# Converting float64 words with an integer add on GpSimd, a planner that keeps VectorE's and GpSimd's SBUF steps apart, and scores in two half banks

## Chip, cores and metric

The kernel runs on one core of one Trainium2 chip. The metric is the device time of one execution in microseconds (us), lower is better. An execution is also recorded by the hardware profiler; its span is the time from the first to the last recorded instruction.

## What is computed

Three parts follow one another. The first is attention within chunks of 64 tokens, for 8 batches, 8 heads and 576 tokens of 64 numbers. The second is a soft mixture of experts on the 4608 x 512 result, with 8 experts of 4 slots. The third is a dense layer of 512 to 2048 with softplus, and one back to 512.

```python
scores = scale * np.matmul(q_c, k_c.transpose(0, 1, 2, 4, 3))   # chunks of 64
attn = np.exp(scores - np.max(scores, axis=-1, keepdims=True))
out = np.matmul(attn / (np.sum(attn, axis=-1, keepdims=True) + 1e-09), v_c)
...
logits = x @ phi                                     # 4608 x 32
d = softmax(logits, over tokens)                     # dispatch
slot_input = (d.T @ x).reshape(8, 4, 512)
slot_out[e] = np.maximum(slot_input[e] @ w1[e], 0.0) @ w2[e]
x = softmax(logits, over slots) @ slot_out           # combine
...
h = x @ w_in
g = np.maximum(h, 0.0) + np.log1p(np.exp(-np.abs(h)))
return (g @ w_out).astype(np.float32)
```

The weights w_in (512 x 2048) and w_out (2048 x 512) come as float64. The kernel loads each number as two 32-bit words, a low and a high one, and makes a float32 of the pair on the chip. One such conversion is of a tile of 128 x 512 numbers; there are 16 of w_in, called wi(c, kt) for quarter c of the 2048 hidden columns and row tile kt, and 16 of w_out, wo0 to wo15, four for each quarter.

## The kernel before

Engines are TensorE (PE), VectorE (DVE), ScalarE (ACT), GpSimd (POOL) and SyncE (SP), which issues all DMAs.

**How the order is made.** The work is cut into named steps. Each step has a cost per engine that may run it (table `COST`), steps that it needs, buffers that it takes and gives back, and a rank. `issue()` (from line 66) is a list scheduler that runs at build time: it keeps a clock for each engine, picks the step that can begin first and emits its instructions. The result is one fixed order for each engine, and on the chip each engine runs its order in line and waits where an operand is not there. A different cost, rank, buffer count or choice of engine changes the orders.

**Stage 1, attention and dispatch (0 to 188.4 us).** There are 36 units of 128 tokens by 512 numbers. For a unit u, PE transposes q and k (L389), ACT copies them to SBUF (B, L401), and PE forms the scores (S, L414: 16 products of 64 x 64 into one PSUM tile of two banks, of which 256 columns each are used). VectorE takes the row maxima (m0, L426) and subtracts them (m1, L432), ACT takes the exponential (x, L439), PE transposes the result (C, L447), ACT copies it out (Ce, L452), PE multiplies by v (D, L466), VectorE normalises (L480, L481, L489), PE transposes back (E, L501) and VectorE copies (Ee, L508). Steps F follow for groups of units and add up logits and slot inputs. There is one score buffer (`S=1`).

**Stage 2, experts (188.4 to 247 us).** PE runs the 16 steps H (w1, L909) and the 16 steps SO (w2), for which weights are streamed in. Beside them the combine weights are made (c1 to c6 and d, L783 to L832; GpSimd makes `cr` at L819 and L820) and the conversions of wi0 and wo0 to 3 run. Then VectorE divides by the sums (so0, L958), PE transposes (soT, L967) and quarter 0 of w_in is folded with the expert results into a table Tc (Td L988, wa L1014, wd L1018).

**Stage 3, the dense layers (from 247 us).** There are 72 steps: 18 token tiles t of 256 by four quarters qd. A step n is: h on PE (L1059, four products 128 x 256 into one of two PSUM tiles `ph`), a sign bit on VectorE (ab, L1072), softplus on ACT (L1078), a maximum and sum on VectorE (mx, L1082), a rounded copy on ACT (pa, L1088), the remainder on GpSimd (pb, L1092), and o on PE: 24 products 128 x 512, eight each at L1109, L1111 and L1113, with w_out held as a rounded and a low part. Sums leave PSUM through oc: a first copy on ACT (L1122) or a sum on VectorE (L1125). The order of steps is: quarter 0 of tiles 0 to EARLY - 1, quarter 1 of the same tiles, quarters 0 and 1 of the others tile by tile, then quarters 2 and 3. EARLY is 4, so step 4 is the first that needs quarter 1 of the table (conversions of wi1, then Tp L996, V L1002, U L1006, wa, wd) and wo4 to 7.

**A conversion before.** For the high word: shift and mask into `cvt` (cb0, L319, VectorE), add the sign (cb1, L322, VectorE), cut the exponent out (cb2, L325, VectorE). ACT squares the high word into `cvm` (cx0, L331) and converts the low word to a float (cx1, L333). Then low times exponent and plus `cvt` (cp0 and cp1, both L847, on VectorE or GpSimd), and a guard that makes tiny numbers zero (cg, L345, VectorE). For w_out there follow a rounded cast (ch, L862, ACT or VectorE) and the low part (cl, L866, GpSimd or VectorE). Two buffer sets `cv` exist at first, four once pool `cvb` opens.

Of the kernel before, what the change touches and what calls it, by code (L numbers as in the profile page):

```python
# [29 lines left out]

COST = {
# [96 lines left out]
def kernel(  # L128
# [711 lines left out]
    def st_cx(k, raw, step, e, held):  # L840
        cv_low(V["cv", k], *words(raw()), step)

    def st_cp(k, raw, step, e, held):
        c = V["cv", k]
        lo, hi = words(raw())
        t = c["t"].bitcast(F32)
        tt(e)(out=t if step else lo, in0=lo, in1=t if step else hi,  # L847
              op=ALU.add if step else ALU.mult)

    def st_cg(k, e, held):  # L850
        c = V["cv", k]
# [507 lines left out]
```

## Time and profile before

| | us |
|---|---|
| runs shown | 719.05, 724.36, 725.68 |
| median | 724.36 |
| the profiled execution | 725.34 |
| its span | 723.6 |

The span is 1.74 us shorter than the profiled execution's own time, which is 0.98 above the median. Times in the rows are microseconds from the span's start. In a row of the timeline stand the start, the duration, the engine, the line of the kernel, the operation, output and inputs by the program's names with shape and type, and a count; in brackets the engine's idle time before the row and what ended it. PEclk is the granted clock of TensorE as a share of 2.4 GHz.

### The profile page before, as it was taken

Reading aid. Unit: us, or ns where it says so; the run is one execution under the profiler, and the core shown is the slowest. Engines: PE = TensorE matmul, PEld = TensorE weight load, DVE = VectorE, ACT = ScalarE, POOL = GpSimd, SP = SyncE. Lnnn points to the kernel's source line nnn. Section 1 sums busy time; section 2 is a strip of 40 time slices with the busy share of each in tenths; the row PEclk is TensorE's granted clock in tenths of the full one; section 3 lists DMA queues with packets and bytes.
Section 4 is the critical chain, followed back from the end, with each engine's and each line's share of the span. In section 5 each row is a group of like instructions: output and inputs, shape, how many; then the busy total and the mean of one; then the engine's idle time right before and its main releaser. Section 6 shows DMA issues by size and latency. Waiting matters only on the chain.

```text
span 723.6 us, 14059 instructions
## 1 busy us (share of the span) xinstructions
PE 659.5 (91%) x5831; PEld 519.2 (72%) x5831; DVE 482.4 (67%) x650; ACT 366.8 (51%) x549; POOL 269.1 (37%) x176
## 2 busy tenths in 40 slices
PE   5998988898997786699999999899999999999997
PEld 4776766676544565488687887788888888888886
DVE  1676877766268799869999899954455555554541
ACT  3897887794046365535455455554333333333330
POOL 2000000000146566645455666753444444333331
PEclk8899999999899799599999999999999999999999
DMA  8898999998499605012323001021323132323222
GB/s 171 225 260 233 284 292 256 297 289 336 186 409 414 266 29 172 32 59 106 127 88 116 30 30 59 30 88 58 116 62 113 64 112 73 102 73 101 73 73 58
DMA packets 79582, 107.92 MB, mean 149 GB/s; under 512 B 41888, under 2 KB 60320, under 8 KB 77216
## 3 DMA queue, kind: packets, MB, share of 16 engines
q1 hardware_dynamic: 79520, 107.04, 46.6%
q8 instruction: 46, 0.75, 0.4%
q14 instruction: 16, 0.13, 0.1%
HBM read 88.15 MB, written 18.87 MB: 148 GB/s over the span
## 4 chain that ended last, share of the span: by engine, by line
PE 62%; DVE 19%; ACT 6%; issue 6%; POOL 4%; SPq 1%; DMA 1%; DVEq 0%; POOLq 0%; ACTq 0%
PE trm L1113 13%; PE trm L1109 13%; PE trm L1111 13%; PE ph L1059 3%; ACT T L401 3%; PE tr L389 3%; PE X L466 3%; PE S L414 2%; PE hps L909 2%; DVE cvt L319 2%; PE tr L501 2%; PE tr L447 2%; DVE cvt L322 2%; DVE cvt L345 2%; DVE hTm L1082 2%
## 5 line engine op out<-in xcount | busy, mean ns | idle before, releaser
L1092 POOL TENSOR_TENSOR g<-hTm,g 128x1024 fp32r<-128x1024 f32 (+2 forms) x50 | 115.9, 2320 | 121.1 <-ACT g L1088 117.3
L401 ACT COPY T<-tr 64x512 f32<-64x512 f32 x144 | 89.6, 622 | 18.9 <-PE tr L389 16.9
L1078 ACT ACTIVATE hTm<-hTm 128x1024 f32<-128x1024 f32 (+2 forms) x51 | 51.5, 1011 | 82.8 <-DVE hTm L1072 82.3
L1088 ACT CAST g<-hTm 128x1024 fp32r<-128x1024 f32 (+2 forms) x51 | 51.0, 999 | 73.1 <-DVE hTm L1082 71.8
L1072 DVE TENSOR_SCALAR hTm<-ph 128x1024 uint32<-128x1024 uint32 (+2 forms) x51 | 59.0, 1158 | 39.8 <-PE ph L1059 39.7
L1092 POOL TENSOR_TENSOR g<-siT,g 128x1024 fp32r<-128x1024 f32 (+1 forms) x25 | 59.0, 2358 | 51.4 <-ACT g L1088 51.3
L1082 DVE SCALAR_TENSOR_TENSOR hTm<-ph,hTm 128x1024 f32<-128x1024 f32 (+2 forms) x51 | 59.0, 1159 | 26.0 <-ACT hTm L1078 25.9
L755 POOL MEMSET siT<- 128x1152 f32 x1 | 1.1, 1057 | 182.2 <-PE tr L577 182.2
L1059 PEld LDWEIGHTS ph<-cT,Tc 128*128 128x128 f32 x288 | 45.2, 197 | 20.9 <-issue 6.6
L1059 PE MATMUL ph<-cT,Tc 128*128 128x256 f32 x288 | 49.6, 297 | 10.0 <-DVE hTm L1082 5.5
L1125 DVE TENSOR_TENSOR i<-trm,i 128x512 f32<-128x512 f32 x44 | 30.2, 687 | 33.7 <-PE trm L1113 33.7
L1078 ACT ACTIVATE siT<-siT 128x1024 f32<-128x1024 f32 (+1 forms) x25 | 25.7, 1027 | 42.2 <-DVE siT L1072 42.1
L1072 DVE TENSOR_SCALAR siT<-ph 128x1024 uint32<-128x1024 uint32 (+1 forms) x25 | 29.5, 1179 | 22.3 <-PE ph L1059 22.3
L1088 ACT CAST g<-siT 128x1024 fp32r<-128x1024 f32 (+1 forms) x25 | 25.4, 1015 | 32.8 <-DVE siT L1082 27.4
L426 DVE TENSOR_REDUCE nm<-S 128x8 f32<-128x512 f32 x36 | 24.8, 690 | 24.5 <-PE S L414 24.1
L1082 DVE SCALAR_TENSOR_TENSOR siT<-ph,siT 128x1024 f32<-128x1024 f32 (+1 forms) x25 | 29.5, 1179 | 15.4 <-ACT siT L1078 15.4
L389 PE MATMUL tr<-ident,q 128*128 128x128 f32 x144 | 30.8, 297 | 4.7 <-DMA q<-in_q_dram 3.8
L414 PE MATMUL S<-T 64*64 64x64 f32 x1152 | 27.7, 228 | 7.2 <-issue 3.0
L414 PEld LDWEIGHTS S<-T 64*64 64x64 f32 x1152 | 22.6, 138 | 13.7 <-issue 10.0
L389 PE MATMUL tr<-ident,k 128*128 128x128 f32 x144 | 28.9, 284 | 1.8 <-DMA k<-in_k_dram 1.8
L508 DVE COPY xT<-tr 128x512 f32<-128x512 f32 x36 | 24.7, 687 | 7.8 <-PE tr L501 7.8
L452 ACT COPY P<-tr 128x512 f32<-128x512 f32 x36 | 21.1, 585 | 16.2 <-PE tr L447 15.6
(449 smaller groups left out, 1807.3 us busy)
## 6 DMA issues: line engine op xcount, KB each, us to landing
part<-i SPq DMA_DIRECT2D x18, 512.0 KB, 2.6
i<-part SPq DMA_DIRECT2D x18, 512.0 KB, 3.8
q<-in_q_dram SPq DMA_DIRECT2D x16, 512.0 KB, 4.6
k<-in_k_dram SPq DMA_DIRECT2D x16, 512.0 KB, 5.6
i<-in_moe_w_dram SPq DMA_DIRECT2D x8, 1024.0 KB, 12.0
vbm<-in_v_dram SPq DMA_DIRECT2D x40, 128.0 KB, 5.6
g<-in_moe_w_dram SPq DMA_DIRECT2D x5, 1024.0 KB, 8.4
...
```

Of the source, the lines that this page charges most:

```text
L389: nc.tensor.transpose(c, t[:, 2 * (u % 2) + h, 2 * rr:2 * rr + 2, :].rearrange("p r d -> p (r d)"), ident)
L401: on(e)(out=t[64 * h:64 * h + 64, :, r2, :], in_=p[64 * r2:64 * r2 + 64])
L414: nc.tensor.matmul(out=sp[64 * o:64 * o + 64, b, 64 * i:64 * i + 64], lhsT=qT[64 * h:64 * h + 64, cs], rhs=kT[64 * h:64 * h + 64, cs], sta ...
L1059: nc.tensor.matmul(out=ph(n, a, b)[:, j - a, :], lhsT=K["Tc"][:, f * 128:(f + 1) * 128], rhs=K["cT"][:, t * TT:(t + 1) * TT], start=True, ...
L1072: nc.vector.tensor_scalar(out=scratch(n, a, b).bitcast(U32), in0=ph(n, a, b).bitcast(U32), scalar1=0x80000000, scalar2=None, op0=ALU.bitwi ...
L1078: nc.scalar.activation(out=y, in_=y, func=AF.Softplus)
L1082: nc.vector.scalar_tensor_tensor(out=y, in0=ph(n, a, b), scalar=0.0, in1=y, op0=ALU.max, op1=ALU.add)
L1088: nc.scalar.copy(out=V["gs", n][:, 0, a:b], in_=scratch(n, a, b))
L1092: tt(e)(out=s[:, 1, a:b], in0=scratch(n, a, b), in1=s[:, 0, a:b].bitcast(F32), op=ALU.subtract)
L1109: nc.tensor.matmul(out=po, lhsT=s[:, 0, j, ts_], rhs=wr[:, hs], start=(n in begin and j == 0), stop=False)
L1111: nc.tensor.matmul(out=po, lhsT=s[:, 0, j, ts_], rhs=wr[:, ls], start=False, stop=False)
L1113: nc.tensor.matmul(out=po, lhsT=s[:, 1, j, ts_], rhs=wr[:, hs], start=False, stop=(j == 3 and n in finish))
```

## The change

- A conversion is now: cb0 and cb1 as before (VectorE); cx0 and cx1 turn the low word into an integer of three bits by scaling it with 2^-29, adding 2^23 and taking 2^23 off again (ACT, two passes, in place); cx2 squares the high word in place (ACT); cb2 is the guard and multiplies `cvt` by 1 or 0 (VectorE); cg adds low word and `cvt` as uint32 (GpSimd, always). cp0 and cp1 are gone, `cvm` and pool `cvb` too; there are four `cv` sets from the start.
- `issue()` has a further clock, `port`: a step whose name is in `PORT` and that runs on VectorE or GpSimd begins no earlier than the last such step ended, on either engine, in the plan. `COST` is retuned, Ce and the first copy in oc may also go to VectorE.
- EARLY is 6. Ranks of late conversions come from a table `need`.
- Scores: one PSUM tile of two banks; a unit takes 256 columns of each bank, and `S=2`. Warm-up products W take no score buffer.

Counts in the two programs: conversion passes on VectorE go from 4 x 32 plus ten cp, four cl and two ch to 3 x 32 plus eleven ch; on GpSimd from 38 cp and 12 cl to 32 cg and 16 cl; on ACT from 64 to 96, and 5 ch for 14. Of 36 Ce, 17 go to VectorE; of 36 first copies, 10 do.

```diff
-EARLY = 4
+EARLY = 6
...
-    "cb0": {"DVE": 0.65}, "cb1": {"DVE": 0.74}, "cb2": {"DVE": 0.55}, "cx0": {"ACT": 0.68},
-    "cx1": {"ACT": 0.68}, "cp0": {"DVE": 0.7, "POOL": 1.4}, "cp1": {"DVE": 0.7, "POOL": 1.4},
-    "cg": {"DVE": 0.87}, "ch": {"ACT": 0.62, "DVE": 0.68}, "cl": {"DVE": 0.7, "POOL": 1.3},
+    "cb0": {"DVE": 0.45}, "cb1": {"DVE": 0.7}, "cb2": {"DVE": 0.7}, "cx0": {"ACT": 0.68},
+    "cx2": {"ACT": 0.68},
+    "cx1": {"ACT": 0.68}, "cg": {"POOL": 1.35}, "ch": {"ACT": 0.62, "DVE": 0.7},
+    "cl": {"DVE": 0.7, "POOL": 1.3},
...
+PORT = {"cb0", "cb1", "cb2", "cl", "pb", "c42", "cg", "c6"}
...
+                if s.nm in PORT and e != "ACT":
+                    t = max(t, port)
...
+        if s.nm in PORT and e != "ACT":
+            port = clock[e]
...
         else:
-            nc.vector.tensor_scalar(
-                out=hi, in0=c["t"], scalar1=0xFF800000, scalar2=None, op0=ALU.bitwise_and)
-
-    def cv_low(c, lo, hi, step):
+            t = c["t"].bitcast(F32)
+            nc.vector.scalar_tensor_tensor(
+                out=t, in0=hi, scalar=TINY2, in1=t, op0=ALU.is_ge, op1=ALU.mult)
+
+    def cv_low(lo, hi, step):
         if step == 0:
-            c["m"] = cv_tile(c, "cvm", F32)
-            nc.scalar.activation(out=c["m"], in_=hi, func=AF.Square)
+            nc.scalar.activation(out=lo, in_=lo.bitcast(U32), func=AF.Copy, scale=2.0 ** -29,
+                                 bias=2.0 ** 23)
+        elif step == 1:
+            nc.scalar.activation(out=lo.bitcast(U32), in_=lo, func=AF.Copy, bias=-2.0 ** 23)
         else:
-            nc.scalar.activation(out=lo, in_=lo.bitcast(U32), func=AF.Copy, scale=2.0 ** -52)
+            nc.scalar.activation(out=hi, in_=hi, func=AF.Square)
...
+    s2 = psa.tile([128, 2, 512], F32, name="S")
...
-            sp = V["S", u] = psa.tile([128, 2, 512], F32, tag="S", name="S")
+            j = held["S", u]
+            sp = V["S", u] = s2[:, :, 256 * j:256 * j + 256]
...
-    clock = issue(steps, dict(BUF, tr=4, S=1, X=1, dT=1))
+    clock = issue(steps, dict(BUF, tr=4, S=2, X=1, dT=1))
...
+        nc.gpsimd.tensor_tensor(out=dst, in0=words(raw())[0].bitcast(U32), in1=t, op=ALU.add)
...
-            nc.scalar.copy(out=hold[t][:, 512 * i:512 * i + 512], in_=po)
+            on(e)(out=hold[t][:, 512 * i:512 * i + 512], in_=po)
...
+    need = {1: (0, 0.5), 2: (EARLY + 4, 0.7), 3: (EARLY + 7, 0.7)}
```

How the orders move is shown at three places, each from the program before and then from the changed one, whose lines are numbered a little differently. The first is VectorE at the end of stage 2, up to the division L958 (L956 in the changed kernel); `cvt` is a conversion's buffer, w1a and w1b are raw halves of w_out. Before:

```order
L345 SCALAR_TENSOR_TENSOR cvt_3698<-cvm_3712,cvt_3698 128x512
L345 SCALAR_TENSOR_TENSOR cvt_3734<-cvm_3741,cvt_3734 128x512
L322 SCALAR_TENSOR_TENSOR cvt_3758<-w1b,cvt_3758 128x512
L866 TENSOR_TENSOR w1a<-cvt_3734,w1a 128x512
L325 TENSOR_SCALAR w1b<-cvt_3758 128x512
L345 SCALAR_TENSOR_TENSOR cvt_3758<-cvm_3766,cvt_3758 128x512
L958 TENSOR_SCALAR ts<-sops_3335,rz 128x256
```

The changed order at the same place:

```order
L327 TENSOR_SCALAR cvt_3752<-w1a 128x512
L327 TENSOR_SCALAR cvt_3755<-w1b 128x512
L330 SCALAR_TENSOR_TENSOR cvt_3752<-w1a,cvt_3752 128x512
L330 SCALAR_TENSOR_TENSOR cvt_3755<-w1b,cvt_3755 128x512
L334 SCALAR_TENSOR_TENSOR cvt_3752<-w1a,cvt_3752 128x512
L334 SCALAR_TENSOR_TENSOR cvt_3755<-w1b,cvt_3755 128x512
L956 TENSOR_SCALAR ts<-sops_3292,rz 128x256
```

The guard L345, which reads what GpSimd wrote, stood in front of the division; in the changed order the steps in front read raw words, `cvt` and ACT's squares alone.

The second place is GpSimd from the last conversions of wi1 (w4b, w5b before) to the low part of wo7 (w3b). L847 is a multiply or add of a conversion, L866 a low part, L1092 a subtract pb of stage 3. Before:

```order
L1092 TENSOR_TENSOR g_4039<-hTm,g_4039 128x1024
L847 TENSOR_TENSOR w5b<-w5b 128x512
L847 TENSOR_TENSOR w2a<-w2a 128x512
L847 TENSOR_TENSOR cvt_4042<-w2a,cvt_4042 128x512
L847 TENSOR_TENSOR cvt_4075<-w2b,cvt_4075 128x512
L866 TENSOR_TENSOR w2a<-cvt_4042,w2a 128x512
L866 TENSOR_TENSOR w2b<-cvt_4075,w2b 128x512
L847 TENSOR_TENSOR w3b<-w3b 128x512
L847 TENSOR_TENSOR cvt_4139<-w3b,cvt_4139 128x512
L866 TENSOR_TENSOR w3a<-cvt_4135,w3a 128x512
L866 TENSOR_TENSOR w3b<-cvt_4139,w3b 128x512
L1092 TENSOR_TENSOR g_4210<-hTm,g_4210 128x1024
```

The changed order, with L855 the integer add and L1090 the subtract pb, from wo4 on:

```order
L855 TENSOR_TENSOR cvt_4034<-w2a,cvt_4034 128x512
L1090 TENSOR_TENSOR g_4091<-siT,g_4091 128x1024
L866 TENSOR_TENSOR w2a<-cvt_4034,w2a 128x512
L855 TENSOR_TENSOR cvt_4095<-w2b,cvt_4095 128x512
L866 TENSOR_TENSOR w2b<-cvt_4095,w2b 128x512
L855 TENSOR_TENSOR cvt_4143<-w3a,cvt_4143 128x512
L1090 TENSOR_TENSOR g_4201<-hTm,g_4201 128x1024
L866 TENSOR_TENSOR w3a<-cvt_4143,w3a 128x512
L1090 TENSOR_TENSOR g_4222<-hTm,g_4222 128x1024
L855 TENSOR_TENSOR cvt_4146<-w3b,cvt_4146 128x512
L1090 TENSOR_TENSOR g_4237<-siT,g_4237 128x1024
L866 TENSOR_TENSOR w3b<-cvt_4146,w3b 128x512
```

The subtracts of later steps now stand between the conversions of wo4 to 7; ahead of the last row there are nine steps' subtracts, before there were four.

The third place is VectorE in stage 1, with the engine that a row waits for in brackets. Before, over two units:

```order
L426 TENSOR_REDUCE nm<-S 128x8 [waits PE_49]
L480 TENSOR_SCALAR z<-X 128x8 [waits PE_49]
L481 RECIPROCAL z<-z 128x8 [waits DVE_49]
L432 TENSOR_TENSOR P<-S,nm 128x512 [waits Activation_49]
L489 TENSOR_TENSOR x<-X,z 128x4x128 [waits DVE_49]
L426 TENSOR_REDUCE nm<-S 128x8 [waits PE_49]
```

The changed order, where L436 takes the maxima, L442 subtracts them and L518 copies out a transposed result:

```order
L442 TENSOR_TENSOR P<-S,nm 128x512 [waits PE_49]
L436 TENSOR_REDUCE nm<-S 128x8
L518 COPY xT<-tr_792 128x512 [waits PE_49]
L490 TENSOR_SCALAR z<-X 128x8 [waits PE_49]
L491 RECIPROCAL z<-z 128x8 [waits DVE_49]
L442 TENSOR_TENSOR P<-S,nm 128x512 [waits PE_49]
```

The subtraction of a unit now waits for PE, which has written the next unit's scores into the other half by then, and the maxima of that next unit need no wait of their own. 11 of the 36 subtractions carry such a wait, none did before.

## Rows read from the trace of the kernel before

**Rows 1.** The page, busy time of each engine: us, share, instructions.
```profile
PE 659.5 (91%) x5831; PEld 519.2 (72%) x5831; DVE 482.4 (67%) x650; ACT 366.8 (51%) x549; POOL 269.1 (37%) x176
```

**Rows 2.** Busy time by stretch, all engines; the first row names the columns.
```profile
core 0: us, PE busy (x) PEld busy (x) DVE busy (x) ACT busy (x) POOL busy (x), PEclk, DMA share, GB/s
0.00:188.40 188.40, 160.26 (x3299) 124.45 (x3299) 119.93 (x269) 139.15 (x258) 5.19 (x32) 0.95 0.92 269
188.40:247.00 58.60, 48.28 (x456) 26.01 (x456) 38.89 (x65) 20.90 (x37) 28.69 (x22) 0.85 0.87 345
247.00:257.60 10.60, 7.66 (x40) 7.05 (x41) 7.67 (x14) 4.96 (x12) 6.33 (x5) 0.83 0.18 60
257.60:283.70 26.10, 25.57 (x114) 19.36 (x112) 25.81 (x34) 16.51 (x29) 17.22 (x13) 0.94 0.19 61
283.70:302.20 18.50, 6.33 (x19) 4.29 (x20) 18.09 (x17) 10.87 (x16) 10.73 (x8) 0.62 0.32 113
302.20:500.00 197.80, 192.40 (x883) 155.02 (x883) 162.85 (x150) 99.62 (x127) 114.92 (x64) 0.99 0.20 72
```

**Rows 3.** Timeline of PE, three rows where idle stretches and waits end.
```profile
246.98 1.89 PE L967 MATMUL trm<-rep,ts 128*128 128x128 f32 x8 [4.59 <-DVE ts L958]
...
289.26 1.22 PE L1006 MATMUL trm<-ts,rep 128*128 128x512 f32 x1 [5.62 <-ACT ts L1002]
...
302.15 0.63 PE L1109 MATMUL trm<-w2a,g 128*128 128x512 f32 x1
```

**Rows 4.** Timeline of VectorE and GpSimd, 243 to 247 us, the division L958 with its forerunners.
```profile
243.40 1.04 POOL L847 TENSOR_TENSOR w1b<-w1b 128x512 f32<-128x512 f32 x1 [0.97 <-DVE w1b L325]
244.52 1.29 POOL L847 TENSOR_TENSOR cvt<-w1b,cvt 128x512 f32<-128x512 f32 x1
245.84 0.69 DVE L345 SCALAR_TENSOR_TENSOR cvt<-cvm,cvt 128x512 f32<-128x512 f32 x1 [2.52 <-POOL cvt L847]
246.45 0.48 DVE L958 TENSOR_SCALAR ts<-sops,rz 128x256 f32<-128x256 f32 x1
```

**Rows 5.** Timeline, single passes of VectorE and GpSimd after 270 us.
```profile
270.51 0.42 DVE L319 TENSOR_SCALAR cvt<-w5b 128x512 uint32<-128x512 uint32 x1
...
276.08 0.68 DVE L322 SCALAR_TENSOR_TENSOR cvt<-w2a,cvt 128x512 uint32<-128x512 uint32 x1
...
297.00 1.27 POOL L866 TENSOR_TENSOR w3b<-cvt,w3b 128x512 fp32r<-128x512 f32 x1 [1.28 <-ACT w3b L862]
...
301.04 2.37 POOL L1092 TENSOR_TENSOR g<-hTm,g 128x1024 fp32r<-128x1024 f32 x1 [2.77 <-ACT g L1088]
...
361.22 2.41 POOL L1092 TENSOR_TENSOR g<-siT,g 128x1024 fp32r<-128x1024 f32 x1
361.30 2.88 DVE L345 SCALAR_TENSOR_TENSOR w4a<-cvm,cvt 128x512 f32<-128x512 f32 x1 [1.46 <-POOL cvt L847]
```

**Rows 6.** Timeline of PE over one step; then busy time of L1109 by stretch.
```profile
505.75 0.64 PE L1059 MATMUL ph<-cT,Tc 128*128 128x256 f32 x4
506.23 0.39 PE L1109 MATMUL trm<-w4a,g 128*128 128x512 f32 x1
...
511.70 0.28 PE L1059 MATMUL ph<-cT,Tc 128*128 128x256 f32 x1
...
302.20:500.00 197.80, 97.48 (x248) 0.99 0.20 72
```

**Rows 7.** Timeline of VectorE, the last sum.
```profile
719.01 0.69 DVE L1125 TENSOR_TENSOR i<-trm,i 128x512 f32<-128x512 f32 x1 [2.03 <-PE trm L1113]
```

**Rows 8.** SP's issue of the last w2 load; DMA issues by target, KB, us to landing.
```profile
222.19 0.33 SPq L283 DMA_DIRECT2D w7b<-in_moe_w_dram  x1
...
w7b<-in_moe_w_dram SPq DMA_DIRECT2D x2, 512.0 KB, 13.1
```

**Rows 9.** Waits before 188.4 us: us in total, times, longest.
```profile
DVE nm L426 <- PE S L414: 24.1, 20, 8.9
...
PE S L414 <- DVE P L432: 1.9, 2, 1.6
```

More of the change, by code (lines that the diff above doesn't have):

```diff
@@ L71, in issue @@
     clock = clock or {e: 0.0 for e in ("SP", "PE", "POOL", "ACT", "DVE", None)}
+    port = 0.0
     free = {b: [(0.0, i) for i in range(n)] for b, n in buffers.items()}
@@ L420, in scores @@
     def scores(u):
-        return V["S", u][:, :, 0:256].rearrange("p b (c k) -> p b c k", k=CH)
+        return V["S", u].rearrange("p b (c k) -> p b c k", k=CH)
     def st_m0(u):
@@ L685, in st_W @@
     def st_W(e, held):
-        p = psa.tile([128, 2, 512], F32, tag="S", name="S")
         for _ in range(2):
-            nc.tensor.matmul(out=p[:, 0, 0:128], lhsT=ident, rhs=ident, start=True, stop=True)
+            nc.tensor.matmul(out=s2[:, 0, 0:128], lhsT=ident, rhs=ident, start=True, stop=True)
     for nm, key, n in (("D", NU - 2, 1), ("D", NU - 1, 2), ("E", NU - 1, 1), ("F", G, 3),
@@ L693 @@
             w = ("w", nm, key, i)
-            add("W", w, st_W, [(nm, key), ("S", NU - 1)], [("S", w)], [("S", w)], NU + 1.0)
+            add("W", w, st_W, [(nm, key), ("m1", NU - 1)], (), (), NU + 1.0)
     def at(f, *a):
@@ L759, in diag @@
         return t.rearrange("p k (e z) -> p k e z", z=NS + SPE)[:, :, :, 0:SPE]
-    cvp.extend((cv_a, i) for i in range(2))
+    cvp.extend((cv_a, i) for i in range(4))
     steps = []
@@ L840, in st_cx, with st_cg @@
     def st_cx(k, raw, step, e, held):
[L841 to L851, printed above, removed]
-        t = c["t"].bitcast(F32)
-        if k[0] == "wo":
-            cv_guard(t, c["m"], t)
-        else:
-            cv_guard(w_in_of(k[1], k[2]), c["m"], t)
+        cv_low(*words(raw()), step)
+    def st_cg(k, raw, e, held):
+        t = V["cv", k]["t"]
+        dst = t if k[0] == "wo" else w_in_of(k[1], k[2]).bitcast(U32)
+        nc.gpsimd.tensor_tensor(out=dst, in0=words(raw())[0].bitcast(U32), in1=t, op=ALU.add)
+        if k[0] != "wo":
             V.pop(("cv", k))
@@ L921, in st_open @@
         K["soT"] = keep.tile([128, KD, 4, NS], F32, name="soT")
-        cv_b = ctx.enter_context(tc.tile_pool(name="cvb", bufs=1, reuse_waits="tile"))
-        cvp.extend((cv_b, i) for i in range(2))
     def st_hs(e, held):
@@ L1152 @@
     ds = [n for n, sl in enumerate(W1) if sl[0] == "d"]
-    add("open", 0, st_open, [("H", n) for n in ds], (), [("cv", "o2"), ("cv", "o3")], 5)
+    add("open", 0, st_open, [("H", n) for n in ds], (), (), 5)
     add("hs", 0, st_hs, [("H", n) for n in range(16)] + start_, (), (), 9)
@@ L1217, in conv, with conv_wi @@
         else:
-            add("cg", k, st(st_cg, k), [("cp1", k), ("cx0", k), ("wia", k[1])], (),
+            add("cg", k, st(st_cg, k, raw), [("cb2", k), ("cx1", k), ("wia", k[1])], (),
                 [("cv", k)] + slot_, r)
-    def conv_wi(c, r):
+    def conv_wi(c, r, step=0.1):
         add("wia", c, st(st_wia, c), [("lw", ("wi", c, 1))], [(WI[c][1], ("wf", c))], (), r)
@@ L1225, in conv_wi @@
                 ("cg", ("wi", c, kt - 1))] * (kt % 2),
-                 r, [(WI[c][0][kt // 2], ("wi", c))] if kt % 2 else [])
+                 r + step * kt, [(WI[c][0][kt // 2], ("wi", c))] if kt % 2 else [])
     def conv_wo(h, r):
@@ L1241 @@
     first = {qd: min(n for n, x in enumerate(order) if x[1] == qd) for qd in range(4)}
+    need = {1: (0, 0.5), 2: (EARLY + 4, 0.7), 3: (EARLY + 7, 0.7)}
     for c in range(4):
-        r = 20 if c == 0 else U0 + first[c] - (0.5 if c == 1 else (30, 28)[c - 2])
-        if c:
-            conv_wi(c, r)
-            add("Tp", c, st(st_Tp, c), sT + [("cg", ("wi", c, kt)) for kt in range(4)],
-                [(mt, ("tp", c))], [(WI[c][1], ("wf", c))], r)
-            add("V", c, st(st_V, c), [("Tp", c)], (), [(mt, ("tp", c))], r)
-            add("U", c, st(st_U, c), [("V", c)], [(mt, ("U", c))], (), r)
-            add("wa", (c, 0), st(st_wa, c, 0, 4), [("U", c)], (), (), r)
-            add("wd", (c, 0), st(st_wd, c, 0, 4), [("wa", (c, 0))], (), [(mt, ("U", c))], r)
-        for h in range(4 * c, 4 * c + 4):
-            conv_wo(h, r + 0.1 * (h % 4 + 1) + (8 if c > 1 else 0))
+        if c == 0:
+            for h in range(4):
+                conv_wo(h, 20.1 + 0.1 * h)
+            continue
+        n, d = need[c]
+        conv_wi(c, U0 + n, d)
+        r = U0 + n + 4 * d
+        add("Tp", c, st(st_Tp, c), sT + [("cg", ("wi", c, kt)) for kt in range(4)],
+            [(mt, ("tp", c))], [(WI[c][1], ("wf", c))], r)
+        add("V", c, st(st_V, c), [("Tp", c)], (), [(mt, ("tp", c))], r)
+        add("U", c, st(st_U, c), [("V", c)], [(mt, ("U", c))], (), r)
+        add("wa", (c, 0), st(st_wa, c, 0, 4), [("U", c)], (), (), r)
+        add("wd", (c, 0), st(st_wd, c, 0, 4), [("wa", (c, 0))], (), [(mt, ("U", c))], r)
+        if c == 1:
+            for h in range(4, 8):
+                conv_wo(h, U0 + 2 + 0.5 * (h - 4))
+    for i, h in enumerate((10, 11, 14, 15, 12, 13, 8, 9)):
+        conv_wo(h, U0 + EARLY + 11 + i)
     for j in range(3):
@@ L1319 @@
     held.update({(W2[n], "w2"): 0 for n in range(5)})
-    held.update({("cv", "o2"): 2, ("cv", "o3"): 3})
     bufs = {sl: 0 for sl in W1 + W2 if sl[0] != "d"}
-    bufs.update({"mt": 4, "cv": 2, "cc": 1, "cr": 1, "ph": 2, "scr0": 1, "scr1": 1, "scr2": 1, "hold": 0})
+    bufs.update({"mt": 4, "cv": 4, "cc": 1, "cr": 1, "ph": 2, "scr0": 1, "scr1": 1, "scr2": 1, "hold": 0})
     held.update({("hold", f"{j}{h}"): 2 * j + i for j in range(3) for i, h in enumerate("ab")})
-    late.sort(key=lambda k: (k[0], (k[1] - 10) % 8 if k[0] == "wo" else 0) if k[0] == "wo" else ("a", k))
     for i, k in enumerate(late):
```

22 lines of the change are left out of this document (9 added, 13 removed), and 6 rows, old and new, of the table COST.

## Prediction

> **What bounds the kernel now.** I read the busy line of the page first: PE is busy 91% of the span [rows 1]. So only its idle stretches can shrink, and the next view, busy time by stretch, says where they are [rows 2]. From 302.2 on PE has next to no idle time (192.40 of 197.80 us, then all of it); until 188.4 it is busy 160.26 of 188.40 us while the DMA engines run at a share of 0.92; the holes lie in 188.4 to 247 (48.28 of 58.60) and above all in 283.7 to 302.2, where PE works 6.33 of 18.50 us and its granted clock, after those idle stretches, is 0.62, a mean between its two levels (1.0 is 2.4 GHz, 0.5 is 1.2). The timeline of PE at these holes [rows 3] names who ends the waits: at 246.98 soT waits 4.59 us for VectorE's L958, at 289.26 U waits 5.62 us for a conversion chain, and the first o step of quarter 1 (step 4 in the order) starts at 302.15.
>
> What stands behind both is one resource. In 243 to 247 [rows 4] VectorE's guard L345 waits 2.52 us for GpSimd's add L847, and L958, which needs nothing of the conversion, is queued behind it. At 361.22 and 361.30 [rows 5] a guard of 0.68 us that starts 0.08 us after a GpSimd subtract of 2.41 us takes 2.88 us: it ends 0.55 us after the subtract. So the two engines' SBUF steps run one after the other. I call their sum port time. From 247 to 302.2 GpSimd is busy 6.33 + 17.22 + 10.73 = 34.3 us, 33 without the 1.2 of its last subtract [rows 2, 5]. VectorE's part is eight conversions (wi1 and wo4 to 7) of 0.42 + 0.68 + 0.42 + 0.68 [rows 5], 17.6, and four multiplies or adds of 0.68, 2.7. That is 53 us of port time in 54 us: the stretch is full, and PE gets its data when the port is done. (VectorE's L1072 and L1082, one operand in PSUM, are not in that sum.)
>
> **The price of a step.** From 505.75 to 511.70 [rows 6] one step of the last stage takes 5.95 us with PE never idle: 0.48 of h and 5.47 of o. From 302.2 to 500 PE runs 248 of the first products of o (8 a step): 31 steps, which at 5.95 are 184.5 of 197.8. 13.3 are lost, 2.6 of them (my estimate from the 1.22 and neighbours at L1006) Tp and U of two quarters, so some 11 to waits. Tried on before: 302.15 + 68 x 5.47 + 64 x 0.48 + 2.6 + 11 = 718.4; the last sum starts at 719.01 [rows 7] and the span ends at 723.6, 5.2 after the model's end; the execution has 1.7 outside its span (725.3).
>
> **The change, part by part.**
>
> *The conversion.* Before: four VectorE steps and a GpSimd multiply and add, 2.20 + about 2.6 = 4.8 us of port time. After: TS, STT, STT (0.42 + 0.68 + 0.68) and one integer add on GpSimd. Nothing in the trace is an integer add there. Bounds: 1.04, the fastest GpSimd pass over 128x512 [rows 4], and 2.37, a pass over twice the elements [rows 5]. I take 1.3, the L847 add and the L866 subtract of that size. Sum 3.08, 1.7 less per conversion. ACT gets a third pass, 32 more in all, less 17 + 10 + 9 that leave it; it is busy half the time [rows 2], so nothing is charged.
>
> *The queue ahead of L958.* In the new order L958 follows steps that wait for no GpSimd step. What is late next is the weight of the last SO: its load is issued at 222.19 and lands 13.1 us later [rows 8], 235.3. With the last SO, L958 and soT behind it I put soT at about 239 against 246.98: 3 to 10 us, taken as 7 to 8. The price if the cover goes (a conversion still stands in front) is 4.6.
>
> *EARLY 6 and the planner's port clock.* Two more steps of quarter 0 (5.47 each, 4 more h of 0.48) run before PE needs quarter 1. In GpSimd's new row nine subtracts stand ahead of the last low part of wo7, instead of four. Port time until step 6 (first of quarter 1) can start: 8 x 1.78 on VectorE, 8 x 1.3 adds, 4 x 1.27 low parts, 9 x 2.37 subtracts = 14.2 + 10.4 + 5.1 + 21.3 = 51; carried over from stage 2 an add and two low parts, 3.9: 55. From 240 a port without a gap ends at 295. PE itself could be there at 289 to 292 (first o at about 250, 6 x 5.47, ten h, Tp and U). The port was full before, but waits on PSUM and ACT will leave gaps: 295 to 303, I take 300. In before the same point of progress was 302.15 + 2 x 5.47 + 4 x 0.48 = 315.0, so this is worth 15.
>
> *After that.* The other 16 conversions save 16 x 1.7 = 27 us of port time where 11 us are lost to waits. I take half back: 6 lost; bounds 3 and 11.
>
> *Casts and copies on VectorE.* 11 casts (9 more), 10 more first copies L1122, 17 more copies of Ce. A cast of this size lies between 0.42 us, the shortest VectorE pass over 128x512, and the 2.88 of a pass that stands beside a subtract [rows 5]; I take an undisturbed pass, 0.69, since the plan keeps subtracts and conversions apart. In 302.2 to 500 VectorE is busy 162.85 of 197.80 [rows 2]: 19 more passes of 0.69 [rows 4] are 13 us, the 16 conversions there save it 16 x 0.42 = 7, so it keeps some 29 idle. Charged nothing, the idle time is the cover; at 2.88 a cast, 9 x 2.2 = 20 more would use two thirds of it, and a late sum would then hold PSUM.
>
> *Stage 1, half banks and Ce.* PE waited only 1.9 us, twice, for the one score buffer [rows 9], so a second can win no more than 1.9. VectorE gets 17 x 0.69 = 12 on 119.93 of 188.40, ACT loses as much of 139.15. The DMA share of 0.92 leaves little to win. But the order shows that 11 of the 36 subtractions m1 now wait for PE, none before: two halves of one bank are ordered as one buffer. I take 0, from -5 to +5.
>
> The Trainium skill (PSUM — Partial Sum Buffer, "PSUM bank collisions raise a hardware error") says that two engines may not be in the same bank and 32-partition quadrant at once, whatever columns they touch. By that rule the half banks give no overlap, and those 11 waits are the price; no run here shows a collision. It is the page behind rival D, whose price is worked out from rows below.
>
> **Sum.** 300 + 66 x 5.47 + 60 x 0.48 + 2.6 + 6 = 698.4; with the 5.2 and 1.7 at the end 705.3 against 725.3 of the same execution, 20 less. The median of the runs is 724.36, 1 us lower; so 704.
>
> **Rivals.**
>
> B, PE never waits: the port keeps ahead because VectorE's three passes start earlier than planned (four cv tiles instead of two in the first part). Step 6 at 289.3 and 3 lost later: 300 - 289.3 + 3 = 13.7 less, 691. For it: the port sum from 240 ends only 3 to 6 us behind PE's own time. Against: before, waits filled the port's gaps everywhere.
>
> C, the integer add is dear, or the port stays as full as before. At 2.37 the add puts 8 x 1.07 = 8.6 on the stretch (step 6 at 309), and the later waits stay 11: 704 + 8.6 + 3 to 5 = 716 to 718. For it: nothing in the trace prices integer work on GpSimd. Against: the price of every 128x512 pass there is 1.04 to 1.39. This is also the case in which the change moves port time about without saving any.
>
> D, the half banks serialise stage 1: m1(u) stands behind S(u+1), which stands behind other PE work, so P(u) and all that follows comes later and PE runs dry. The price is PE work between m0(u) and S(u+1): half a unit, 160.26 / 36 / 2 = 2.2 us, to a whole one, 4.45, in 11 units: 24 to 49 us. It decides (the gain gone) from 20 / 11 = 1.8 us a unit. At 2.2 to 3 a unit the time is 728 to 737. For it: the waits in the order, and that VectorE already waits 24.1 us for S [rows 9]. Against: several transposed units are in flight, and stage 1 is fed by DMA at 0.92.
>
> **How the numbers follow.** My forecast has 0.55 (698 to 711 by its own bounds: port gaps 295 to 303, later waits 3 to 11), B 0.17, C 0.18, D 0.10. A measurement of this kernel tells about 1% from no change, 7.2 us: faster is below 717.1, slower above 731.6. Faster: 0.55 + 0.17 + half of C = 0.81; within 1%: the other half of C and a third of D, 0.12; slower: 0.07. The range goes from B's 691, a little below, to beyond C: 690 to 720; outside it are D and little else on either side.
>
> **What would show it.** Right: soT at 237 to 241; the integer add at 1.2 to 1.4 us; the first o step of quarter 1 at 295 to 303 with six steps done ahead of it and PE's granted clock not down to 0.62 there; 33 to 34 steps between 302 and 500. Wrong: an add over 2 us (C); m1 waiting for S on VectorE's row for more than 20 us in all, and stage 1 ending after 195 (D); step 6 after 310; or soT still after 244, held by another step ahead of L958.

## The result and the profile after

The changed kernel takes 697.92 us (median of four runs) where the kernel before takes 725.02 beside it: a ratio of 0.9652, 95% interval 0.957 to 0.9733. The forecast was 704 in a range of 690 to 720. Ratios, here and below, leave out the executions that lie over 1.5% above the fastest of their kernel (four of ten of the kernel old_conv, 732.44 to 733.5, and one of 2164.81 of the changed kernel when it was run again), and the medians keep them. The profiled execution took 698.02 us, 27.3 less than that of before, with a span of 696.2.

The page's busy line of the changed kernel, to set beside [rows 1]:

```profile
PE 650.9 (93%) x5831; PEld 518.8 (75%) x5831; DVE 436.9 (63%) x638; ACT 370.6 (53%) x546; POOL 254.5 (37%) x163
```

PE does the same 5831 products in 8.6 us less busy time (its mean granted clock is 0.975 where it was 0.959), and VectorE has lost 45 us. The stretches that answer to [rows 2], with the same columns:

```profile
186.30:247.50 61.20, 51.88 (x496) 31.33 (x496) 37.57 (x63) 33.45 (x62) 26.16 (x21) 0.92 0.86 340
247.50:288.30 40.80, 40.25 (x179) 31.28 (x180) 36.96 (x50) 32.39 (x50) 29.05 (x20) 0.96 0.31 103
288.30:296.20 7.90, 3.47 (x17) 2.85 (x16) 7.67 (x8) 5.84 (x7) 7.90 (x5) 0.79 0.00 0
296.20:500.00 203.80, 203.80 (x948) 167.81 (x948) 129.97 (x140) 103.79 (x129) 111.68 (x58) 0.99 0.23 81
```

The hole of 18.5 us is one of 7.9, and behind it PE has no idle time up to 500 us, while VectorE's load there is down to 130 of 204 us. In the timeline, soT, the end of the last wait, the first o of quarter 1 and the last sum (before: [rows 3, 7]):

```profile
237.12 1.16 PE L965 MATMUL trm<-rep,ts 128*128 128x128 f32 x8 [2.37 <-DVE ts L956]
...
294.00 2.41 PE L1057 MATMUL ph<-cT,Tc 128*128 128x256 f32 x8 [3.57 <-DVE siT L1080]
...
296.21 0.63 PE L1107 MATMUL trm<-w2a,g 128*128 128x512 f32 x1
...
691.66 0.69 DVE L1123 TENSOR_TENSOR i<-trm,i 128x512 f32<-128x512 f32 x1 [2.03 <-PE trm L1111]
```

I cut the time at four marks, all starts of such rows: the end of stage 1 (the products at L770, L779 after), soT, the first o of quarter 1, the last sum. To compare the third stretch, two steps (2 x 5.47 and four h of 0.48, 12.9 us) are moved from the last stretch to the third where EARLY is 4.

| stretch | before | after | difference | forecast |
|---|---|---|---|---|
| to the end of stage 1 | 188.39 | 186.35 | -2.0 | 0 |
| to soT | 58.59 | 50.77 | -7.8 | -7 to -8 |
| to the first o of step 6 | 55.17 + 12.9 | 59.09 | -9.0 | the rest of -15 |
| to the last sum | 416.86 - 12.9 | 395.45 | -8.5 | -5 |

### The profile page after: what moved, and what is told of

It reads as the page before. It is cut to its first block, busy times and chain, and to the rows that moved or that the text cites. A ratio compares the mean times of both kernels' runs of the same rounds, so it can differ in the third digit from the quotient of the medians.

```text
span 696.2 us, 13993 instructions
## 1 busy us (share of the span) xinstructions
PE 650.9 (93%) x5831; PEld 518.8 (75%) x5831; DVE 436.9 (63%) x638; ACT 370.6 (53%) x546; POOL 254.5 (37%) x163
## 4 chain that ended last, share of the span: by engine, by line
PE 82%; DVE 5%; DMA 5%; ACT 3%; issue 3%; SPq 1%; POOL 0%; ACTq 0%; POOLq 0%; DVEq 0%
PE trm L1111 19%; PE trm L1107 19%; PE trm L1109 19%; PE ph L1057 5%; PE tr L398 4%; DMA k<-in_k_dram 3%; PE X L476 3%; PE S L424 2%; PE tr L457 2%; PE tr L511 2%; PE sops L946 2%; PE tr L529 1%; PE tr L587 1%; ACT T L410 1%; DMA q<-in_q_dram 1%
## 5 line engine op out<-in xcount | busy, mean ns | idle before, releaser
L1090 POOL TENSOR_TENSOR g<-hTm,g 128x1024 fp32r<-128x1024 f32 (+2 forms) x51 | 118.6, 2326 | 118.1 <-ACT g L1086 114.9
L1070 DVE TENSOR_SCALAR hTm<-ph 128x1024 uint32<-128x1024 uint32 (+2 forms) x51 | 59.0, 1159 | 49.6 <-PE ph L1057 49.6
L1086 ACT CAST g<-hTm 128x1024 fp32r<-128x1024 f32 (+2 forms) x51 | 50.9, 998 | 56.9 <-DVE hTm L1080 53.0
L1090 POOL TENSOR_TENSOR g<-siT,g 128x1024 fp32r<-128x1024 f32 (+1 forms) x25 | 58.1, 2326 | 57.9 <-ACT g L1086 52.7
L1080 DVE SCALAR_TENSOR_TENSOR hTm<-ph,hTm 128x1024 f32<-128x1024 f32 (+2 forms) x51 | 59.1, 1160 | 30.6 <-ACT hTm L1076 30.3
L1123 DVE TENSOR_TENSOR i<-trm,i 128x512 f32<-128x512 f32 x48 | 33.0, 687 | 41.3 <-PE trm L1111 41.3
L1070 DVE TENSOR_SCALAR siT<-ph 128x1024 uint32<-128x1024 uint32 (+1 forms) x25 | 29.5, 1180 | 26.8 <-PE ph L1057 25.8
L1080 DVE SCALAR_TENSOR_TENSOR siT<-ph,siT 128x1024 f32<-128x1024 f32 (+1 forms) x25 | 29.5, 1179 | 13.2 <-ACT siT L1076 13.2
L436 DVE TENSOR_REDUCE nm<-S 128x8 f32<-128x512 f32 x36 | 24.7, 686 | 15.3 <-PE S L424 15.2
L442 DVE TENSOR_TENSOR P<-S,nm 128x512 f32<-128x512 f32 x36 | 24.6, 683 | 7.8 <-PE S L424 7.1
L518 DVE COPY xT<-tr 128x512 f32<-128x512 f32 x36 | 24.7, 685 | 5.7 <-PE tr L511 5.7
```

Source lines behind the costliest of these rows:

```text
L1070: nc.vector.tensor_scalar(out=scratch(n, a, b).bitcast(U32), in0=ph(n, a, b).bitcast(U32), scalar1=0x80000000, scalar2=None, op0=ALU.bitwi ...
L1080: nc.vector.scalar_tensor_tensor(out=y, in0=ph(n, a, b), scalar=0.0, in1=y, op0=ALU.max, op1=ALU.add)
L1086: nc.scalar.copy(out=V["gs", n][:, 0, a:b], in_=scratch(n, a, b))
L1090: tt(e)(out=s[:, 1, a:b], in0=scratch(n, a, b), in1=s[:, 0, a:b].bitcast(F32), op=ALU.subtract)
```

## The experiments

This table holds the marks of every profile that is read below. "From stage 1" is the last sum less the end of stage 1. A row's marks are of one execution.

| kernel | median us | stage 1 ends | soT | first o of quarter 1 (step) | last sum | from stage 1 |
|---|---|---|---|---|---|---|
| before | 725.02 | 188.39 | 246.98 | 302.15 (4) | 719.01 | 530.6 |
| changed | 697.92 | 186.35 | 237.12 | 296.21 (6) | 691.66 | 505.3 |
| only_conv | 707.09 | 183.25 | 240.19 | 290.65 (4) | 700.85 | 517.6 |
| only_early6 | 721.56 | 187.24 | 246.06 | 312.48 (6) | 717.71 | 530.5 |
| old_conv | 727.86 | 190.75 | 241.72 | 326.33 (6) | 726.40 | 535.7 |
| early4 | 704.58 | 184.98 | 236.68 | 291.01 (4) | 698.83 | 513.9 |
| no_port | 701.03 | 186.55 | 241.42 | 301.98 (6) | 697.30 | 510.8 |
| double_pool | 710.31 | 185.01 | 237.57 | 302.98 (6) | 704.81 | 519.8 |
| o6_first | 695.51 | 183.29 | 234.57 | 287.62 (6) | 688.65 | 505.4 |
| full_bank | 693.31 | 184.05 | 234.75 | 292.67 (6) | 686.93 | 502.9 |
| full_bank_again | 697.60 | 182.65 | 233.33 | 292.36 (6) | 687.78 | 505.1 |
| best | 699.17 | 182.02 | 232.45 | 285.41 (6) | 686.46 | 504.4 |
| copies_act | 700.62 | 190.66 | 243.93 | 303.38 (6) | 698.64 | 508.0 |

Before, only_conv and only_early6 have one and the same order on VectorE in stage 1, and yet that stage ends between 183.25 and 188.39; the changed kernel, early4, no_port, double_pool and o6_first share another and end between 183.29 and 186.55, and old_conv, with that same order, at 190.75 in its execution of 732.75 us. So the end of stage 1 moves by 3 to 7 us without an edit, and the last column is the one to compare. It moves by itself too: full_bank and full_bank_again are one program and differ there by 2.2 us.

### The conversion alone

The kernel before takes over `cv_bits`, `cv_low`, `st_cx`, `st_cg`, the steps of `conv` and their costs from the changed kernel, and nothing else:

```diff
-        add("cp0", k, st(st_cp, k, raw, 0), [("cb2", k), ("cx1", k)], (), (), r)
-        add("cp1", k, st(st_cp, k, raw, 1), [("cp0", k)], (), (), r)
+        add("cx2", k, st(st_cx, k, raw, 2), [("cb1", k)], (), (), r)
+        add("cb2", k, st(st_cb, k, raw, 2), [("cx2", k)], (), (), r)
...
+            add("cg", k, st(st_cg, k, raw), [("cb2", k), ("cx1", k)], (), (), r)
```

> The kernel before with the new conversion alone (integer add on GpSimd, costs of its steps, its buffers in the two pools as before); EARLY 4, no port clock, one score buffer. Port theory (the stretch before quarter 1 is as long as VectorE's and GpSimd's conversion and subtract passes laid end to end): 8 x 1.7 = 14 us less port time, the first o step of quarter 1 at 286 to 290 instead of 302, and later waits shrink by some 5: 703 to 709. Filler theory (PE only lacked two more steps of quarter 0 to do; the conversion's own price hardly counts): within 5 of before, 719 to 724. Queue theory (the gain is the division L958 standing free of GpSimd): here a cast and a low part that wait for GpSimd's add stand ahead of it again, so soT stays at 244 to 247 and the time gains only what the port gives.

Measured 707.09, ratio to before 0.9797 (0.9754 to 0.9841). From stage 1 it is 13.0 us shorter. PE at the start of quarter 1:

```profile
283.48 2.08 PE L1054 MATMUL ph<-cT,Tc 128*128 128x256 f32 x8 [5.61 <-DVE Tc L1013]
...
288.50 2.35 PE L1054 MATMUL ph<-cT,Tc 128*128 128x256 f32 x8 [2.94 <-DVE hTm L1077]
290.65 0.63 PE L1104 MATMUL trm<-w2a,g 128*128 128x512 f32 x1
```

The same waits as before stand there, earlier. soT comes 56.9 us after stage 1 against 58.6, so the queue theory is right that the conversion alone does little there; soT's 240.19 itself is below its 244 to 247 only because stage 1 ended early. 4.7 us are won from soT to step 4, 6.7 after it. The time of 707.09 lies in the port theory's range, but its size for the first stretch does not hold: 290.65 comes near its 286 to 290 because stage 1 ended 5.1 us earlier, and from the end of stage 1 the first o step comes 6.4 us earlier (107.4 against 113.8), where 14 us less port time had been counted.

### EARLY 6 alone

```diff
-EARLY = 4
+EARLY = 6
```

> The kernel before with EARLY 6 alone. Port theory: 53 us of port time plus the subtracts of five more steps, 5 x 2.37 = 12, is 65 from 247, so the first o step of quarter 1 (now step 6) starts at 312 to 316, where the same point of progress was 315.0 before: 721 to 726, no gain. Filler theory: PE uses the 16 us it lost for the two steps, step 6 at 302 to 306: 711 to 716.

Measured 721.56, ratio 1.0003 (0.9971 to 1.0035); from stage 1 0.1 us less. The filler theory falls:

```profile
301.89 2.05 PE L1006 MATMUL trm<-ts,rep 128*128 128x512 f32 x2 [7.06 <-ACT w3b L862]
...
310.36 2.33 PE L1059 MATMUL ph<-cT,Tc 128*128 128x256 f32 x8 [2.94 <-DVE hTm L1082]
312.48 0.63 PE L1109 MATMUL trm<-w2a,g 128*128 128x512 f32 x1
```

PE does its two steps, but the wait comes back whole. The steps bring VectorE's sign bits and maxima and GpSimd's subtracts with them, and these stand among the conversions of quarter 1; which of the two it is that delays these, this run does not tell.

### All but the conversion

The changed kernel gets back the conversion of before, with its guard, costs and buffer pools; its multiply and add count as port steps:

```diff
-PORT = {"cb0", "cb1", "cb2", "cl", "pb", "c42", "cg", "c6"}
+PORT = {"cp0", "cp1", "cb0", "cb1", "cb2", "cl", "pb", "c42", "cg", "c6"}
...
+        add("cp0", k, st(st_cp, k, raw, 0), [("cb2", k), ("cx1", k)], (), (), r)
+        add("cp1", k, st(st_cp, k, raw, 1), [("cp0", k)], (), (), r)
```

> The changed kernel with the old conversion (its multiply and add counted as port steps, buffers opened as before), all other edits kept: EARLY 6, port clock, half banks, copies on VectorE. Port theory: 51 + 8 x 1.7 = 65 us of port time plus what is carried over from stage 2 (an old conversion costs more there too, 6 to 8) from 240: step 6 at 310 to 315 instead of 296, later waits up by some 6: 716 to 724. Filler theory: the two steps cover it, 700 to 706. Planner theory (the port clock and the order free of waits made the gain, whatever the conversion): 698 to 704.

The ratio to before is 1.0037 (1.0002 to 1.0071), so some 724: the top of what the port theory gave, and far from the planner theory. By the median of the table, 727.86, it would be 0.9% above the 721.46 of before. Its profile is of an execution of 732.75 us, above its median, so I take from it only where PE waits. Columns of the first row as in [rows 2]:

```profile
302.00:330.00 28.00, 13.22 (x44) 10.66 (x44) 21.20 (x24) 16.03 (x19) 22.77 (x14) 0.50 0.11 41
...
326.33 0.63 PE L1118 MATMUL trm<-w2a,g 128*128 128x512 f32 x1
```

PE is at its lower level for 28 us and starts step 6 at 326, later than the 310 to 315 I gave. Seven h stand one behind the other there, before the first o, with six waits of 1.81 to 2.90 us for VectorE's L1091 to free a `ph` buffer.

### EARLY 4 in the changed kernel

```diff
-EARLY = 6
+EARLY = 4
```

> The changed kernel with EARLY 4, all else kept. Port theory: five subtracts fewer stand before the first step of quarter 1, 12 us, so the conversions are through at 281 to 284 instead of 293 to 298; PE, with two steps less to do, is there at 275 and waits. Step 4 at 282 to 287; the same point of progress in the changed kernel is 296.2 - 12.9 = 283.3. Total within 4 of the changed kernel: 696 to 702. Filler theory (the two steps are what filled the hole): 11 to 13 lost, 707 to 711.

Measured 704.58, 8.6 us more from stage 1 than the changed kernel: neither theory's range. GpSimd does come free sooner, it idles 4.22 us up to 283.38, but PE stands at a third place:

```profile
281.71 1.20 PE L1057 MATMUL ph<-cT,Tc 128*128 128x256 f32 x4 [3.66 <-DVE hTm L1080]
...
288.29 1.20 PE L1057 MATMUL ph<-cT,Tc 128*128 128x256 f32 x4 [3.65 <-DVE hTm L1080]
...
291.01 0.63 PE L1107 MATMUL trm<-w2a,g 128*128 128x512 f32 x1
```

Several h of quarter 1 stand ahead of its first o, and each waits for VectorE's L1080 to release one of two `ph` buffers; after these waits PE is at its lower level (granted clock 0.50 from 281 to 291; 0.43 us from one o product to the next at 291, 0.23 at full clock). So the port is not what holds step 4 here. EARLY 6 is worth 8.6 us with the new conversion by these marks, 7 by the ratios (0.9748, 0.9708 to 0.9788, against 0.9652), and nothing in the kernel before.

### Without the port clock

```diff
-PORT = {"cb0", "cb1", "cb2", "cl", "pb", "c42", "cg", "c6"}
+PORT = set()
```

> The changed kernel without the port clock in the planner; conversions, EARLY 6, half banks and costs kept. Port theory: the chip makes the two engines take turns whether the plan knows it or not; what changes is the order. A cast and a low part that wait for GpSimd's add stand ahead of the division again (soT at 239 to 245 instead of 237), and passes that stand beside each other take 1.8 to 2.9 us instead of 0.7: 698 to 706. Planner theory (the clock is where the gain comes from): most of the 27 us goes, 712 or more.

Measured 701.03; from stage 1 5.5 us more than the changed kernel. 4.1 of them are at soT, 54.9 after stage 1 instead of 50.8, where the division starts at

```profile
240.88 0.48 DVE L956 TENSOR_SCALAR ts<-sops,rz 128x256 f32<-128x256 f32 x1 [7.05 <-PE sops L946]
```

and waits for PE's last SO, which was itself held back 3.7 us by transposes (L835) that wait for GpSimd's `cr`. So the clock acts through the order that it makes. What it is worth stays unclear: the profile is of the slowest of four executions (703.63), the medians differ by 3.1, and the intervals overlap (0.964 to 0.9749 against 0.957 to 0.9733). Most of the gain stays without it, so the planner theory falls.

### A second GpSimd pass behind each integer add

```diff
+        hi = words(raw())[1]
+        nc.gpsimd.tensor_tensor(out=hi, in0=hi, in1=hi, op=ALU.add)
```

> The changed kernel with a second GpSimd pass of the same size behind every integer add (it doubles the squared high word, which nothing reads any more). Port theory: 8 x 1.3 = 10 us more before step 6, and the four of wo0 to 3 carry over a part: step 6 at 304 to 312 instead of 296.2; later waits up by 2 to 5: 708 to 718. Slack theory (GpSimd is busy 37% of the span, so a pass more there is hidden): 697 to 701.

Measured 710.31, 14.5 us more from stage 1 than the changed kernel, inside the port theory's range; the ratio to before is 0.9833 (0.98 to 0.9867), and the slack theory falls. One of the added passes (L857), a cast behind another one, and the start of step 6:

```profile
269.50 1.04 POOL L857 TENSOR_TENSOR w5b<-w5b 128x512 f32<-128x512 f32 x1
...
277.86 2.60 DVE L864 CAST w2a<-cvt 128x512 fp32r<-128x512 f32 x1 [2.21 <-POOL w2a L857]
...
302.98 0.63 PE L1109 MATMUL trm<-w2a,g 128*128 128x512 f32 x1
```

The pass costs 1.04, so 8.3 for the eight of quarter 1, and 32 x 1.04 = 33 in all; of those 33 us 14.5 reach the end: 8.1 by step 6, 6.4 after it. But the pass adds more than time on GpSimd or the port: in tiles of w_out the cast L864 writes into the buffer that the pass works on, so it has to wait for the pass. Ten casts do, for 0.9 to 2.7 us each. The run shows that a GpSimd pass per conversion is not hidden; it does not show that the port is the reason.

### o of step 6 ahead of two h

```diff
+    by["h", (EARLY + 4, 0)].after = [by["o", (EARLY, 0)]]
```

> The changed kernel with one rule more: h of step 10 comes after o of step 6 (it stood in front of it, and h of step 11 too). PE's order alone changes. In the changed kernel PE waits 3.6 us for a free ph buffer at 290.4, with o of step 6 behind, whose subtract is done at 289.8. My reading: o of step 6 starts at 290 to 291, waits for the low part of wo7 till 298.7, and 2 to 4 us are won: 694 to 697. Rival (the wait only moves: wo7's low part and the subtracts of steps 10 and 11 come as late as PE saves): 697 to 700.

Measured 695.51, but from stage 1 505.4 against 505.3: the rival is right. o of step 6 starts at 287.62, and then PE waits inside it:

```profile
295.11 0.50 PE L1107 MATMUL trm<-w3b,g 128*128 128x512 f32 x1 [3.21 <-DVE w3b L862]
...
296.46 0.50 PE L1109 MATMUL trm<-w3b,g 128*128 128x512 f32 x1 [0.84 <-POOL w3b L866]
```

wo7 (w3b) comes when VectorE and GpSimd have done it, whatever PE does first. The time itself lies in the range of my reading; only the time from stage 1 decides, in one profile.

### Full banks, and both edits

```diff
-            sp = V["S", u] = s2[:, :, 256 * j:256 * j + 256]
+            sp = V["S", u] = psa.tile([128, 2, 512], F32, tag="S", name="S")
...
-    clock = issue(steps, dict(BUF, tr=4, S=2, X=1, dT=1))
+    clock = issue(steps, dict(BUF, tr=4, S=1, X=1, dT=1))
```

> The changed kernel with one score buffer of two full banks, as before; all else kept. My reading: stage 1 is fed by DMA, PE waited 1.9 us in all for the one buffer: dispatch ends within 2 us of the changed kernel's 186.4, total 696 to 701. Half-bank theory: the second half earned the 2 us by which stage 1 is shorter, or more: dispatch ends at 188.5 to 191, total 700 to 704. Serial theory (the halves order m1 behind the next scores): with one buffer stage 1 is 3 us or more shorter, total under 695.

> The changed kernel itself, beside the next three on one chip. Its stage 1 ended at 183.3 to 186.4 in the runs that share its program for that stage, so the end of stage 1 moves by some 3 us without any edit; total 695 to 700.

> The changed kernel with one score buffer of two full banks, a second time, now beside the changed kernel on the same chip. Scatter theory: the 4.6 us between their medians were the scatter of stage 1: medians within 2 us of each other. Serial theory (the halves order m1 behind the next scores and cost time): 3 us or more below the changed kernel again, 691 to 695 where that has 695 to 700.

> Both edits that looked better than the changed kernel: one score buffer of two full banks, and h of step 10 behind o of step 6. If both hold, 4.6 + 2.4 = 7 below the changed kernel, 689 to 692; if the full banks were scatter, 2 to 3 below it, 693 to 697.

The first time full banks took 693.31, which looked like a gain of 4.6, though the ratio's interval (0.9549 to 0.9662) overlaps that of the changed kernel. On one chip with the changed kernel the two are alike: 697.60 and 697.48, ratios to before 0.9653 (0.9617 to 0.9689) and 0.9645 (0.9607 to 0.9682). Both edits together took 699.17 (0.9667, 0.9616 to 0.9717). So the 4.6 were not seen again, and no version here is shown to beat the changed kernel. What the half banks do in stage 1 of the changed kernel, in the view of waits (before: [rows 9]):

```profile
DVE nm L436 <- PE S L424: 15.2, 10, 9.8
...
DVE P L442 <- PE S L424: 7.1, 8, 1.7
```

The subtraction does wait for the next unit's scores, 7.1 us in eight places, and the maxima wait 9 us less for theirs: VectorE's wait moved from one to the other, 24.1 against 22.3 in all.

### Copies on ACT

```diff
-"Ce": {"ACT": 0.6, "DVE": 0.69}
+"Ce": {"ACT": 0.6}
...
-"oc": {"ACT": 0.6, "DVE": 0.7}
+"oc": {"ACT": 0.6}
```

> The changed kernel with all 36 Ce copies and all 36 first copies of oc on ACT, as before; all else kept. My reading (the copies were charged nothing, VectorE and ACT both have idle time beside them): within 3 us, 695 to 701. Rival (ACT, busy 139 of 188 us in stage 1 of the kernel before, set the pace there): stage 1 ends 3 us or more later, 189 or more, total 701 to 705.

Measured 700.62, ratio to before 0.9701 (0.9663 to 0.9738), whose interval overlaps that of the changed kernel beside it. Stage 1 ended at 190.66 in its profile, as the rival said, but a program with the changed kernel's own stage 1 ended at 190.75 once, so this doesn't decide. 3.1 us lie between the medians and 2.7 from stage 1, which is near the scatter of either; what the copies are worth stays open.

## Why the prediction was right, step by step

**Port time before quarter 1.** The forecast took the stretch as full of port time. Shown is less: the conversion's work on VectorE and GpSimd moves the time. With the cheaper conversion the time falls (only_conv), with a GpSimd pass more it rises (double_pool), and two more steps for PE, which bring passes of both engines, change nothing (only_early6). That it is the port, and not the queue of either engine with what its passes wait for, is not shown. VectorE is as full as the port sum: busy 51.57 of 55.20 us before [rows 2] and 44.63 of 48.70 after (247.5 to 296.2), with its passes on PSUM operands, which the port sum leaves out. Those stand last before step 4 in the kernel before:

```profile
296.31 1.23 DVE L1072 TENSOR_SCALAR hTm<-ph 128x1024 uint32<-128x1024 uint32 x1
297.45 1.22 DVE L1072 TENSOR_SCALAR siT<-ph 128x1024 uint32<-128x1024 uint32 x1
298.65 1.23 DVE L1082 SCALAR_TENSOR_TENSOR hTm<-ph,hTm 128x1024 f32<-128x1024 f32 x1
299.80 1.22 DVE L1082 SCALAR_TENSOR_TENSOR siT<-ph,siT 128x1024 f32<-128x1024 f32 x1
```

GpSimd runs one pass beside them, of 1.27 us at 297.00 [rows 5], so the port was not full there. No run gives VectorE alone more work, which would part the two readings; only_conv, old_conv and early4 each missed a size that the port theory had given. The sum by itself is near the stretch again after the change. VectorE's conversion passes from 247.5 to 296.2, the shifts, the sign and the guard (us of the stretch, busy time and count):

```profile
247.50:296.20 48.70, 2.46 (x6) 0.93 0.26 86
...
247.50:296.20 48.70, 4.94 (x6) 0.93 0.26 86
...
247.50:296.20 48.70, 6.82 (x7) 0.93 0.26 86
```

At undisturbed durations these are 6 x 0.42 + 13 x 0.68 = 11.4 us; GpSimd is busy 29.05 + 7.90 = 37.0 there, a few passes of it drawn out. That is 48.4 of 48.7 us, three casts on VectorE not counted, with a third less work for each conversion. Laid end to end the passes thus fill the stretch before and after, but such a sum does not say that none of them overlapped or waited.

**The integer add costs 1.3.** Of the 32 adds 24 take 1.29 to 1.33, six 1.43 or 1.44 and two 1.71 and 1.75; that it is an integer add makes no difference to GpSimd here (the float add L847 took 1.29 [rows 4]). Rival C falls. The end of stage 2, where two stand beside VectorE's passes:

```profile
234.07 0.68 DVE L334 SCALAR_TENSOR_TENSOR cvt<-w1a,cvt 128x512 f32<-128x512 f32 x1
234.91 1.77 DVE L334 SCALAR_TENSOR_TENSOR cvt<-w1b,cvt 128x512 f32<-128x512 f32 x1 [0.15 <-ACT w1b L344]
236.60 0.47 DVE L956 TENSOR_SCALAR ts<-sops,rz 128x256 f32<-128x256 f32 x1
...
234.83 1.29 POOL L855 TENSOR_TENSOR cvt<-w1a,cvt 128x512 uint32<-128x512 uint32 x1 [1.23 <-DVE cvt L334]
236.75 1.29 POOL L855 TENSOR_TENSOR cvt<-w1b,cvt 128x512 uint32<-128x512 uint32 x1 [0.63 <-DVE cvt L334]
```

**soT.** Forecast at about 239, measured 237.12, and 7.8 us nearer to stage 1, as said. The reason was right but not whole: no wait for GpSimd by semaphore is left in front of the division, yet the guard ahead of it takes 1.77 instead of 0.68 beside the add, and PE still waits 2.37 us for the division.

**Step 6.** Forecast at 295 to 303 with 300 as the value, measured 296.21. What it waits for in the end is not what I named: 3.57 us for a free `ph` buffer, with h of steps 10 and 11 ahead of it, while VectorE runs L1070 and L1080 back to back (291.51 to 295.07). The port sum from 240 to 295 ended with the low part of wo7, and that runs to 298.70, 2.5 us after step 6 began. So the sum came within 1.2 us of step 6 partly by luck. The wait for `ph` covers wo7's, as o6_first shows.

**Later waits.** This is the term that was sized wrong. I took 11 us down to 6. With the 0.6 by which the same formula missed the kernel before (718.4 against 719.01), 296.21 + 66 x 5.47 + 60 x 0.48 + 2.6 + 0.6 is 689.2, and the last sum starts at 691.66: 2.5 are lost. The conversion's saving holds through the whole kernel, and 6.7 of the 8.5 us come with it alone. The forecast's half was a choice without a row, and 2.5 lies just outside its bounds of 3 and 11. In all 27.3 us were won where 20 were forecast: step 6 came 3.8 earlier than the 300 taken for it, 2.0 of them in stage 1, and the later waits are 3.5 shorter. 697.92 is at the very edge of the forecast's own 698 to 711.

**Stage 1.** I took 0; the profile shows 2.0 less, less than the 3 to 7 us by which that stage moves without an edit. The waits of m1 on S that rival D rests on are real (7.1 us), but VectorE gains as much at the maxima. The Trainium skill's rule on banks (PSUM — Partial Sum Buffer, "PSUM bank collisions raise a hardware error"), that two engines may not be in one bank and quadrant at once, fits these waits. The equal times of the two versions do not test it, since PE had waited only 1.9 us for the one buffer [rows 9].

**The parts don't add.** From stage 1, the conversion alone won 13.0, EARLY alone 0.1, and all together 25.3; everything but the conversion won nothing (ratio 1.0037). With the new conversion EARLY 6 is worth 8.6 by the marks and the port clock up to 5.5, which its times do not confirm. That these edits need the time on VectorE and GpSimd that the conversion frees fits all of this, but is argued.

## What to carry to other kernels

Where passes of two engines hold each other up, add up their undisturbed durations over the stretch. A sum near the stretch says that less work on these engines is worth trying, and that filler for the waiting engine may move nothing if it brings work for the same two (0.1 us here). It does not say whether the shared resource, one engine's own queue or the waits between them sets the end: for that, give each engine alone a pass more, and look that no other step waits for that pass. Once there is room, the filler can pay (8.6 us here), so test such edits together and one by one. And before a few us are put down to an edit, look at how far the marks ahead of it move by themselves; the time from the last mark that the edit can't touch is the better measure.

## What had not been expected

Stage 1 ended between 183.25 and 188.39 us in three programs with one and the same order on VectorE there, and between 183.29 and 190.75 in six others, nearly as much as whole executions of one kernel scatter (694.9 to 703.61 for the changed one). And from 228 to 236 VectorE's passes took 1.2 and 1.77 instead of 0.42 and 0.68 although the plan keeps the two engines' port steps apart: the plan's times are not the chip's, and what the plan keeps apart can still meet on the chip.
